# Attention features and a gated feed-forward on one core: tied issue for the gate stage's late work, earlier x rows, fill pieces between the last pairs' products

## The chip, the cores and the metric

The kernel runs on one core of a Trainium2 chip, in one launch. The metric is device time in microseconds; the time before is the median of three runs. A second number, the span, is the time from the first to the last instruction in one profiled execution. Both are lower when better.

## The reference, cut to what matters

```python
def phi(x):                                    # x: [8, 8, 576, 64]
    proj = x @ w_phi                           # [64, 128]
    proj = proj - max(abs(proj), axis=-1)
    return concat([exp(proj), exp(-proj)])
q_p, k_p = phi(q), phi(k)
kv  = einsum('bhsf,bhsd->bhfd', k_p, v);  z = sum(k_p, axis=2)
num = einsum('bhsf,bhfd->bhsd', q_p, kv); den = einsum('bhsf,bhf->bhs', q_p, z) + 1e-06
x   = (num / den) as [4608 tokens, 512]
xn  = x / sqrt(mean(x*x) + 1e-06) * rms_g
g, val = xn @ w_gate, xn @ w_val               # both [512, 1536]
out = (g * sigmoid(g) * val) @ w_out           # [1536, 512]
```

All of it is fp32. Every product is made of three fp32r matmuls over operands that are split into a high and a low half (high by high, high by low, low by high).

## The kernel before, in words

**Three stages follow each other on TensorE.** The *pair stage* (the loop `for i in range(PR + 3)`) treats 32 pairs of heads, each in four steps that are one loop turn apart: `front` (transposes, projection), `mid` (exponentials, the key-value sums), `back` (the query products into the tiles `nd`, then the denominators through DRAM: `dd`, `dr`, reciprocal, `di`, `rc`) and `last` (`nd` times `rc`, written to the DRAM tensor `xs`). `_merge` lays the pieces of these streams into one sequence by their places between 0 and 1.

**Fill pieces.** The first three of the twelve 128-column groups of both feed-forward weights are kept in SBUF (`fg`, `fv`). Their products with the raw x, not yet normalised, are made while the pair stage runs: x is cut in 18 blocks of 256 tokens; `load_x` fetches one by a DMA on ScalarE's queue (line 145), `fill` splits it into the tile `xo` (ScalarE casts the high half at line 60, VectorE subtracts the low half at line 61), and six units (line 482, 12 matmuls of 256 columns each) multiply it. A unit's sum is copied out by ScalarE (`fo`, line 485) and stored to `gvs`. Until the loop is over a unit writes one of the two PSUM tiles of the pool `ps_f` (`fp`); afterwards one of three tiles `sm`. Units are handed out after the streams of a turn by a quota, and all that is left after the loop.

**The gate stage** has 9 blocks of 512 tokens (`bk`). In each, `gv` makes nine column groups j: 12 matmuls for the gate and 12 for the value (line 605), then `hidden` (ScalarE's `sl`, line 588, VectorE's `h`, line 590, a store to `hs`). I call one such group of 24 matmuls a column pair. Three more groups a block come from the fills: `raw_load` fetches `gvr` (line 612), `gv_raw` multiplies it by the row scale `ri` (line 616) and calls `hidden`. Value sums have three PSUM tiles (`gp`); gate sums have three others (`gq`), except in block 0, where they use the two `fp` tiles that the fills use too. The next block's x is fetched (line 145), squared and summed by `prep` (lines 150 to 154, two matmuls with ones at 159 and 160, square root at 162, reciprocal at 163, scaling at 165) and split by `parts` into `xb`. The decoding of w_out (`_decode`, lines 48 to 55) and the making of the output operands (`split_o`, lines 636 to 647, from loads `wc<-wos`) also run here. During block 0 `load_gv` (line 581) loads the weights of columns j + 1 on ScalarE's queue and splits them: high on ScalarE, low on GpSimd.

**The output stage** multiplies `hs` by w_out with seven products per 2 by 2 block (line 777).

**What sets the order.** The program is written out in Python order, and the Tile scheduler then reorders each engine's instructions by a timing model of its own, as dependencies allow. Each engine runs its list in that order, so an instruction that waits holds what stands behind it. `late()` is the kernel's means against early placement: each instruction that it encloses, on ScalarE, VectorE or GpSimd, is made to stand behind the latest instruction written so far on its engine (those that were themselves enclosed are skipped). Before the change it encloses the decoding, the fills' splits, the reciprocal and scaling in `back` and `last`, and the first block's `prep`.

Of the kernel before, what the change touches and what calls it, by code (L numbers as in the profile page):

```python
# [8 lines left out]
F32 = mybir.dt.float32  # L9
# [54 lines left out]
def _merge(streams):  # L64


    todo = []
    for n, st in enumerate(streams):
        for i, piece in enumerate(st):
            at = (i + 0.5) / len(st)  # L70
            if isinstance(piece, tuple):
                at, piece = piece
            todo.append((at, n, i, piece))
    for _, _, _, piece in sorted(todo, key=lambda t: t[:3]):
        piece()


def _spread(pieces, a, b):
    return [(a + (b - a) * (n + 0.5) / len(pieces), p) for n, p in enumerate(pieces)]
# [3 lines left out]
def kernel(ctx: ExitStack, tc: tile.TileContext, q, k, v, w_phi,  # L83
# [13 lines left out]
    J1 = 3  # L97
    T = 512
    NB = N // T
# [48 lines left out]
    def prep(bk, x, pool, name):  # L148
        ss = xm.tile([128, T], F32, name="ss", bufs=1)
        nc.scalar.activation(ss, x[:, 0], AF.Square)  # L150
        for c in range(1, NC):
            sq = xm.tile([128, T], F32, name="sq", bufs=1)
            nc.scalar.activation(sq, x[:, c], AF.Square)
            nc.gpsimd.tensor_tensor(ss, ss, sq, ALU.add)
        sp = pool.tile([128, T], F32, name=name)
        sh = xm.tile([128, T], F32R, name="sq", bufs=1)
        sl = xm.tile([128, T], F32R, name="sl", bufs=1)
        _split(nc, sh, sl, ss, lo_eng=nc.gpsimd)
        nc.tensor.matmul(sp[:, 0:T], ones, sh, start=True, stop=False)
        nc.tensor.matmul(sp[:, 0:T], ones, sl, start=False, stop=True)  # L160
        ri = rip.tile([128, T], F32, name="ri")
        nc.scalar.activation(ri, sp[:, 0:T], AF.Sqrt, scale=1.0 / DM, bias=eps)
        nc.vector.reciprocal(ri, ri)  # L163
        for c in range(NC):
            nc.vector.scalar_tensor_tensor(x[:, c], x[:, c], g[:, c:c + 1], ri, ALU.mult, ALU.mult)  # L165
        return ri

    def parts(bk, x, ri):
        xhl = xops[bk % len(xops)].tile([128, 2, NC, T], F32R, name="xb")
        for c in range(0, NC, 2):  # L170
            _split(nc, *(a[:, c:c + 2] for a in (xhl[:, 0], xhl[:, 1], x)), lo_eng=nc.gpsimd)
        return xhl[:, 0], xhl[:, 1], ri

    ps_f = ctx.enter_context(tc.tile_pool(name="ps_f", bufs=2, space=PSUM))
# [5 lines left out]
    @contextmanager  # L180
    def late():

        ins = nc.cur_bb.bb.instructions
        n = len(ins)
        with ExitStack() as es:
            for eng in LATE:
                for i in reversed(ins[-300:]):
                    if i.engine == eng and i.name not in waiting:
                        es.enter_context(tc.issue_after(i))
                        break  # L190
            yield
        waiting.update(i.name for i in nc.cur_bb.bb.instructions[n:])
# [82 lines left out]
    def load(pr):  # L275
        b, hp = divmod(pr, NP)
        h0 = 2 * hp
        kt = ld.tile([128, 2, T0, D], F32, name="kt")
        qt = ld.tile([128, 2, T0, D], F32, name="qt")
        for dst, src in ((kt, k), (qt, q)):  # L280
            nc.sync.dma_start(out=dst.rearrange("p h t d -> p h (t d)"),
                              in_=src[b, h0:h0 + 2, 0:SM, :].rearrange("h (p t) d -> p h (t d)", t=T0))
        rb = ld.tile([128, 2, D], F32, name="rb")
        vm, vr = vms[pr % 3], vrs[pr % 3]
        for i, src in enumerate((k, q)):
            nc.sync.dma_start(out=rb[:, i], in_=src[b, h0:h0 + 2, SM:S, :])
        for hh in range(2):
            nc.sync.dma_start(out=vm[:, hh, :, 0:D], in_=v[b, h0 + hh, 0:SM, :].rearrange("(p t) d -> p t d", t=T0))
            nc.sync.dma_start(out=vr[hh * 64:(hh + 1) * 64, hh, 0:D], in_=v[b, h0 + hh, SM:S, :])
        st[pr] = dict(kt=kt, qt=qt, rb=rb, hp=hp, b=b, vm=vm, vr=vr, kv=kvs[pr % 2])  # L290
# [174 lines left out]
    fills, ended = [], []  # L465
# [23 lines left out]
    PR = B * NP  # L489
    early, decs_late = decode_jobs()  # L490
    decs = decode_pieces(early, dec)
    RES = 6 * J1 * 2
    units, here = [], []
    dq = quota = 0.0

    def load_x():
        while fills and len(here) < (1 if held else 2):
            bk = fills.pop(0)
            here.append((bk, fetch(bk, TF, nc.scalar)))

    def landed():
        if here:
            units.extend(fill(*here.pop(0)))

    load(0)
    nc.sync.dma_start(out=g, in_=rms_g.rearrange("(c p) -> p c", p=128))
    load(1)
    for i in range(PR + 3):
        streams = []
        if i < PR:  # L510
            streams.append(_spread(front(i), -0.2, 0.7))
        if 0 <= i - 1 < PR:
            streams.append(_spread(mid(i - 1), -0.2, 1.1))
        if 0 <= i - 2 < PR:
            streams.append(back(i - 2))
        if 0 <= i - 3 < PR:
            streams.append(last(i - 3))
        dq += 1
        dl, decs = decs[:int(dq)], decs[int(dq):]
        dq -= int(dq)  # L520
        streams.append(dl)
        _merge(streams)

        if i == PR - 3:
            with late():
                ri0 = prep(0, x0, ps_f, "fp")
        if len(units) <= 3:
            landed()
        if len(units) + (len(fills) + len(here)) * J1 * 2 > RES:
            quota += (N // TF * J1 * 2 - RES) / (PR - 4)  # L530
            nf = int(quota)
            quota -= nf
            now, units[:] = units[:nf], units[nf:]
            _merge([now])
        if i == PR - 5:
            x0 = fetch(0)
            held.append(x0)
        if not PR - 5 <= i < PR - 3:
            load_x()
        if i + 2 < PR:  # L540
            load(i + 2)
# [51 lines left out]
    def gv(bk, j):  # L593
        if bk == 0 and j + 1 < JN:
            load_gv(j + 1)
        xh, xl, _ = xb[bk]
        r = []
        for wi in range(2):
            gp = ps_g.tile([128, 512], F32, name="gp") if wi else ps_h.tile([128, 512], F32, name="gq") if bk else ps_f.tile([128, T], F32, name="fp")
            i = 0  # L600
            pl = place(wi, j)
            for c in range(NC):
                a, al = pl[0][:, c], pl[1][:, c]
                for w, e in ((a, xh), (a, xl), (al, xh)):
                    nc.tensor.matmul(gp[:, 0:T], w, e[:, c], start=(i == 0), stop=(i == 3 * NC - 1))  # L605
                    i += 1
            r.append(gp[:, 0:T])
        hidden(bk, J1 + j, *r)
# [6 lines left out]
    def gv_raw(bk, j, r):  # L615
        nc.vector.tensor_tensor(r, r, xb[bk][2].unsqueeze(1).broadcast_to([128, 2, T]), ALU.mult)  # L616
        hidden(bk, j, r[:, 0], r[:, 1])
# [21 lines left out]
    def split_o(kp, pool, wt):  # L639
        w, t = wt  # L640
        sub = lambda o, a, b: nc.vector.tensor_tensor(t[:, o], a, b, ALU.subtract)  # L641
        sub(0, w[:, 3], w[:, W11])
        sub(2, w[:, W22], w[:, 3])
        sub(1, w[:, W22], t[:, 0])
        sub(3, w[:, W21], t[:, 1])
        wh = pool.tile([128, 7, DH], F32R, name=f"wh{kp}")
        wl = pool.tile([128, 7, DH], F32R, name=f"wl{kp}")
        _split(nc, wh[:, 0:3], wl[:, 0:3], w[:, 0:3])
        _split(nc, wh[:, 3:7], wl[:, 3:7], t)
        return wh, wl  # L650
# [9 lines left out]
    for bk in range(NB):  # L660
        for n, j in enumerate(LAST if bk == NB - 1 else range(JN)):
            gv(bk, j)
            m, k = divmod(n, JN // J1)
            if k == 1:
                gv_raw(bk, m, raw)
            if k == 2 and (m + 1 < J1 or bk + 1 < NB):
                raw = raw_load(bk, m + 1) if m + 1 < J1 else raw_load(bk + 1, 0)
            if n == 1 and bk + 1 < NB:
                xn = fetch(bk + 1)
            if n == JN // 3 and bk + 1 < NB:  # L670
                xb[bk + 1] = parts(bk + 1, xn, prep(bk + 1, xn, *((ps_f, "fp") if bk else (ps_g, "gp"))))
            if bk and n % 2 == 0 and decs:
                decs.pop(0)()
            if wot and n % 4 == 0:
                wos_ops.append(split_o(len(wos_ops), rg, wot))
                wot = None
            if not decs and not wot and len(wos_ops) < PRE and n % 4 == 1:
                wot = fetch_o(len(wos_ops))
# [170 lines left out]
```

## Time and profile before

| | us |
|---|---|
| median of three runs (1323.54, 1328.35, 1331.91) | 1328.35 |
| the profiled execution's own time | 1328.31 |
| its span | 1326.5 |
| TensorE busy in the span | 1281.4 |
| TensorE idle in the span | 45.1 |
| pair stage, up to the last query product | 0 to 492.9 |
| fills left over, block 0 of the gate stage among them | 492.9 to 611.2 |
| gate stage, rest | 611.2 to 1059.9 |
| output stage | 1059.7 to 1326.5 |

Times in the profile are counted from the first instruction. A row of the view of waits names the engine that sat idle, the tile and line it was about to write, and after the arrow what it waited for. In a list of stretches each engine's busy time is followed by its count of instructions; PEclk is the share of TensorE's clock that was granted.

### The profile page before, as it was taken

To read this page: it belongs to the slowest core of one execution; us is meant where nothing else is said; L and a number is where in the kernel's file an instruction comes from. 1 tells how busy PE (TensorE), PEld (TensorE's weight loads), DVE (VectorE), ACT (ScalarE), POOL (GpSimd) and SP (SyncE) were. 2 spreads that over 40 slices of the span, in tenths; PEclk is the share of its full clock that TensorE was granted. 3 is DMA by queue.
4 is the path that set the end of the run, shared out by engine and by line. 5 is a ranking of instruction groups with operands and counts; after the bars stand their busy time and mean duration, and the time that the engine had idled before them with its cause. 6 is when DMAs were issued, how large, how long until landed. Compare 5 with 4: busy or idle time off the path is not lost. (4 is left out here: it accounts for less than half of the span.)

```text
span 1326.5 us, 24218 instructions
## 1 busy us (share of the span) xinstructions
PE 1281.4 (97%) x8886; PEld 1189.3 (90%) x8886; DVE 864.4 (65%) x1228; ACT 701.8 (53%) x1472; POOL 624.8 (47%) x580
## 2 busy tenths in 40 slices
PE   7989999999999998999999999999999999999998
PEld 7989999999999997998888877777888899999998
DVE  7889887888788854113365764656442777678773
ACT  6878886887778874344243332433431444444442
POOL 4666665665566765002321313223310277777773
PEclk9999999999999999999999999999999999999999
DMA  5445575656656337544444535444423544544441
GB/s 161 128 126 151 162 183 172 166 158 169 171 160 190 103 122 222 176 136 136 149 152 140 170 113 178 160 153 136 158 79 124 179 136 144 159 128 154 152 141 48
DMA packets 198229, 197.13 MB, mean 149 GB/s; under 512 B 69024, under 2 KB 154912, under 8 KB 198112
## 3 DMA queue, kind: packets, MB, share of 16 engines
q1 hardware_dynamic: 179104, 181.44, 44.9%
q10 hardware_dynamic: 19008, 14.16, 3.7%
q8 instruction: 70, 1.15, 0.4%
q14 instruction: 47, 0.39, 0.1%
HBM read 126.04 MB, written 69.50 MB: 147 GB/s over the span
## 5 line engine op out<-in xcount | busy, mean ns | idle before, releaser
L388 POOL TENSOR_TENSOR ql<-eq,qh 128x256 fp32r<-128x256 f32 x256 | 217.6, 881 | 55.7 <-issue 30.9
L605 PE MATMUL gp<-xb,wv 128*128 128x512 f32 x648 | 157.8, 392 | 7.3 <-DVE h L590 7.2
L605 PEld LDWEIGHTS gp<-xb,wv 128*128 128x128 f32 x648 | 120.7, 188 | 35.6 <-DVE h L590 11.0
L54 POOL TENSOR_TENSOR wa<-raw,wa 128x192 f32<-128x192 f32 (+1 forms) x112 | 66.4, 613 | 163.4 <-DVE wa L52 94.9
L605 PE MATMUL gq<-xb,wg 128*128 128x512 f32 x576 | 138.5, 390 | 1.4 <-ACT sl L588 1.4
L359 PE MATMUL acc<-vm,ek 128*128 128x65 f32 x1024 | 131.2, 270 | 0.0
L605 PEld LDWEIGHTS gq<-xb,wg 128*128 128x128 f32 x576 | 108.1, 188 | 24.2 <-ACT sl L588 1.8
L359 PEld LDWEIGHTS acc<-vm,ek 128*128 128x128 f32 x1024 | 127.5, 194 | 0.4 <-ACT ek L346 0.2
L323 DVE TENSOR_REDUCE mx<-pp 128x4 f32<-128x512 f32 (+1 forms) x160 | 100.8, 631 | 28.4 <-PE pp L321 26.5
L590 DVE TENSOR_TENSOR h<-sl,gp 128x512 f32<-128x512 f32 x81 | 55.1, 682 | 78.6 <-PE gp L605 50.2
L588 ACT ACTIVATE sl<-gq 128x512 f32<-128x512 f32 x72 | 42.7, 594 | 114.4 <-PE gq L605 85.2
L384 ACT ACTIVATE qh<-sm 128x512 fp32r<-128x512 f32 (+1 forms) x192 | 97.4, 507 | 0.0
L61 POOL TENSOR_TENSOR xb<-x,xb 128x1024 fp32r<-128x1024 f32 x18 | 46.6, 2609 | 105.8 <-ACT xb L60 105.8
L319 PE MATMUL pp<-wh,th 128*128 128x256 f32 x288 | 88.5, 309 | 4.8 <-ACT th L60 1.5
L383 ACT ACTIVATE eq<-sm 128x512 f32<-128x512 f32 x128 | 78.5, 613 | 13.0 <-PE sm L372 9.7
L616 DVE TENSOR_TENSOR gvr<-gvr,ri 128x1024 f32<-128x1024 f32 x27 | 34.9, 1291 | 77.0 <-DMA gvr<-gvs 77.0
L321 PE MATMUL pp<-wh,tl 128*128 128x256 f32 x288 | 84.6, 300 | 0.1
L320 PE MATMUL pp<-wl,th 128*128 128x256 f32 x288 | 81.3, 283 | 0.0
L605 PE MATMUL gp<-xb,fv 128*128 128x512 f32 x324 | 78.1, 390 | 0.0
L346 ACT ACTIVATE ek<-yk 128x512 f32<-128x512 f32 x128 | 75.3, 650 | 1.1 <-DVE yk L326 1.1
L605 PE MATMUL gq<-xb,fg 128*128 128x512 f32 x288 | 70.9, 396 | 1.9 <-ACT sl L588 1.9
L605 PEld LDWEIGHTS gp<-xb,fv 128*128 128x128 f32 x324 | 61.0, 188 | 13.0 <-DVE h L590 0.3
(210 smaller groups left out, 3829.9 us busy)
## 6 DMA issues: line engine op xcount, KB each, us to landing
hs<-h SPq DMA_DIRECT2D x108, 256.0 KB
ht<-hs SPq DMA_DIRECT2D x18, 1536.0 KB
gvs<-fo SPq DMA_DIRECT2D x108, 128.0 KB
gvr<-gvs SPq DMA_DIRECT2D x27, 512.0 KB
rc<-di SPq DMA_DIRECT2D x32, 288.0 KB
x<-xs ACTq DMA_DIRECT2D x18, 512.0 KB
x<-xs SPq DMA_DIRECT2D x9, 1024.0 KB
kt<-in_k_dram SPq DMA_DIRECT2D x32, 256.0 KB
```

The source lines that it names most:

```text
L54: nc.gpsimd.tensor_tensor(a[:, h], lf[:, h], a[:, h], ALU.mult)
L319: nc.tensor.matmul(o, th[:, cs], wh, start=True, stop=False)
L320: nc.tensor.matmul(o, th[:, cs], wl, start=False, stop=False)
L321: nc.tensor.matmul(o, tl[:, cs], wh, start=False, stop=True)
L323: nc.vector.tensor_reduce(mx[:, 0:2 * m], pp[:, 0:2 * m], axis=AX.X, op=ALU.max, apply_absolute_value=True)
L346: nc.scalar.activation(e[h][:, sg], y["k", h], AF.Exp, scale=1.0 - 2.0 * sg)
L359: nc.tensor.matmul(acc[:, sg, h], e[h][:, sg, j], vm[:, h, j], start=False, stop=(h == 1 and j == T0 - 1))
L383: nc.scalar.activation(ei[:, sg], yi, AF.Exp, scale=1.0 - 2.0 * sg)
L384: nc.scalar.activation(hi[:, sg], yi, AF.Exp, scale=1.0 - 2.0 * sg)
L388: nc.gpsimd.tensor_tensor(lo[:, sg, cs], ei[:, sg, cs], hi[:, sg, cs].bitcast(F32), ALU.subtract)
L590: nc.vector.tensor_tensor(h, sl, vr, ALU.mult)
L605: nc.tensor.matmul(gp[:, 0:T], w, e[:, c], start=(i == 0), stop=(i == 3 * NC - 1))
```

## The change

It makes five edits, all of order or of buffers; the arithmetic and the number of instructions on each engine stay the same.

1. `gv_raw`, the later blocks' `prep` and `split_o` are enclosed in `late()`.
2. The next block's x is fetched after column pair 0 instead of 1, and `prep` and `parts` are written after pair 2 instead of 3.
3. In the last two turns of the pair loop a new stream of 8 and 10 calls of `more` lies between 0 and 0.64 of the turn; each makes one fill unit, and splits and loads further x blocks as needed.
4. The quota no longer hands out units in those two turns.
5. The gate sums of block 0 use the three `gp` tiles that the value sums use, no longer the `fp` tiles.

```diff
+    def more():
+        if len(units) <= 3:
+            landed()
+        if units:
+            units.pop(0)()
+        load_x()
...
+        if i > PR:
+            streams.append(_spread([more] * (8 if i == PR + 1 else 10), 0, 0.64))
         _merge(streams)
...
-        if len(units) + (len(fills) + len(here)) * J1 * 2 > RES:
+        if i <= PR and len(units) + (len(fills) + len(here)) * J1 * 2 > RES:
...
-            gp = ps_g.tile([128, 512], F32, name="gp") if wi else ps_h.tile([128, 512], F32, name="gq") if bk else ps_f.tile([128, T], F32, name="fp")
+            gp = ps_g.tile([128, 512], F32, name="gp") if wi else ps_h.tile([128, 512], F32, name="gq") if bk else ps_g.tile([128, 512], F32, name="gp")
...
             if k == 1:
-                gv_raw(bk, m, raw)
+                with late():
+                    gv_raw(bk, m, raw)
...
-            if n == 1 and bk + 1 < NB:
+            if n == 0 and bk + 1 < NB:
                 xn = fetch(bk + 1)
-            if n == JN // 3 and bk + 1 < NB:
-                xb[bk + 1] = parts(bk + 1, xn, prep(bk + 1, xn, *((ps_f, "fp") if bk else (ps_g, "gp"))))
+            if n == 2 and bk + 1 < NB:
+                with late():
+                    rin = prep(bk + 1, xn, *((ps_f, "fp") if bk else (ps_g, "gp")))
+                xb[bk + 1] = parts(bk + 1, xn, rin)
...
             if wot and n % 4 == 0:
-                wos_ops.append(split_o(len(wos_ops), rg, wot))
+                with late():
+                    wos_ops.append(split_o(len(wos_ops), rg, wot))
```

Lines after the new function are numbered 7 to 13 higher in the changed kernel: 588, 590 and 616 become 597, 599 and 625.

**Where the order moves.** The first place is VectorE at the end of the pair stage. `kv1l` is the last pair's key-value sum, `nd` the scaling of a pair that is done, `xo` the low half of a fill block. Before:

```order
L61 TENSOR_TENSOR kv1l<-acc,kv1h 128x4x65
L433 RECIPROCAL dr<-dr 128x9
L450 TENSOR_TENSOR nd<-nd,rc 64x576
L451 TENSOR_TENSOR nd<-nd,rc 64x576
L616 TENSOR_TENSOR gvr<-gvr,ri 128x1024
L61 TENSOR_TENSOR xo<-x,xo 128x512 x2
```

and now:

```order
L61 TENSOR_TENSOR kv1l<-acc,kv1h 128x4x65
L433 RECIPROCAL dr<-dr 128x9
L61 TENSOR_TENSOR xo<-x,xo 128x512 x2
L450 TENSOR_TENSOR nd<-nd,rc 64x576
L451 TENSOR_TENSOR nd<-nd,rc 64x576
L433 RECIPROCAL dr<-dr 128x9
L599 TENSOR_TENSOR h<-sl,gp 128x512
```

The fill block's low half stands ahead of the two scalings, and the first multiplication of `gvr` has left this place.

The second place is VectorE in the middle of the gate stage, the 29th to the 32nd `h` of a column pair (block 3). `wc` and `wl` belong to `split_o`. Before:

```order
L55 TENSOR_TENSOR wa<-wp,wa 128x256
L641 TENSOR_TENSOR wc<-wc 128x256
L590 TENSOR_TENSOR h<-sl,gp 128x512
L590 TENSOR_TENSOR h<-sl,gvr 128x512
L616 TENSOR_TENSOR gvr<-gvr,ri 128x1024
L590 TENSOR_TENSOR h<-sl,gp 128x512
...
L590 TENSOR_TENSOR h<-sl,gp 128x512
L163 RECIPROCAL ri<-ri 128x512
L641 TENSOR_TENSOR wc<-wc 128x256 x2
L61 TENSOR_TENSOR wl_12014<-wc,wh_12013 128x768
L165 SCALAR_TENSOR_TENSOR x<-x,g,ri 128x512 x4
```

and now, from the 29th to the 33rd:

```order
L55 TENSOR_TENSOR wa<-wp,wa 128x256
L599 TENSOR_TENSOR h<-sl,gp 128x512
L625 TENSOR_TENSOR gvr<-gvr,ri 128x1024
L599 TENSOR_TENSOR h<-sl,gvr 128x512
L599 TENSOR_TENSOR h<-sl,gp 128x512 x3
L625 TENSOR_TENSOR gvr<-gvr,ri 128x1024
L163 RECIPROCAL ri<-ri 128x512
L599 TENSOR_TENSOR h<-sl,gvr 128x512
L165 SCALAR_TENSOR_TENSOR x<-x,g,ri 128x512 x4
```

From one multiplication of `gvr` to the next there are now always three `h` of column pairs, where before there were two to four, and the work on `wc` is gone from here: the first four output operands now stand around the 60th to the 73rd `h`, in blocks 6 to 8.

The third place is ScalarE at the end of the pair stage: `wg`, `wv` are the weight tiles of block 0 (their number is the column group), `wc` their loads. Before:

```order
L60 CAST wv_1_9025<-wc 128x512
L485 COPY fo<-fp 128x256
L425 ACTIVATE nd<-sm,epsd 65x288 x2
L581 DMA wc<-wgs 128x4x128
L485 COPY fo<-fp 128x256
L581 DMA wc<-wvs 128x4x128
L485 COPY fo<-fp 128x256
L60 CAST xo<-x 128x512 x2
L60 CAST wg_2_9027<-wc 128x512
L60 CAST wv_2_9029<-wc 128x512
L485 COPY fo<-fp 128x256
L145 DMA x<-xs 128x4x256
```

and now:

```order
L60 CAST wv_1_9025<-wc 128x512
L485 COPY fo<-fp 128x256
L145 DMA x<-xs 128x4x256
L485 COPY fo<-fp 128x256
L425 ACTIVATE nd<-sm,epsd 65x288 x2
L590 DMA wc<-wgs 128x4x128
L590 DMA wc<-wvs 128x4x128
L60 CAST wg_2_9027<-wc 128x512
L485 COPY fo<-fp 128x256
L60 CAST wv_2_9029<-wc 128x512
L485 COPY fo<-fp 128x256
L590 DMA wc<-wgs 128x4x128
```

The load of the next x block moves ahead of the weight loads, the casts of `xo` have left (they now stand ahead of the first weight's cast), and the casts of the third weights stand between the fills' copies.

## The prediction

> **What bounds the kernel now.** I read the busy shares first, then the same by stretches that follow the stages.
>
> ```profile
> PE 1281.4 (97%) x8886; PEld 1189.3 (90%) x8886; DVE 864.4 (65%) x1228; ACT 701.8 (53%) x1472; POOL 624.8 (47%) x580
> ```
>
> ```profile
> 493.70:560.00 66.30, 60.23 (x459) 58.34 (x458) 21.73 (x21) 29.14 (x67) 21.65 (x14) 0.97 0.67 208
> 560.00:610.00 50.00, 50.00 (x402) 49.18 (x402) 6.90 (x10) 20.06 (x48) 7.47 (x6) 1.00 0.44 140
> 610.00:760.00 150.00, 150.00 (x669) 124.44 (x668) 82.94 (x105) 56.84 (x95) 43.34 (x39) 1.00 0.45 150
> 760.00:930.00 170.00, 159.48 (x683) 128.22 (x682) 99.03 (x139) 57.77 (x98) 45.56 (x48) 0.99 0.44 147
> 930.00:1060.00 130.00, 130.00 (x576) 107.72 (x576) 63.21 (x67) 40.00 (x58) 22.29 (x11) 1.00 0.40 136
> ```
>
> TensorE (PE) is the bound. In these rows (time, busy time and count of PE, PEld, DVE, ACT and POOL, PE's granted clock, DMA) it has no gap in three stretches of the part that the change reorders; two have holes: 493.7 to 560 (fills and block 0) and 760 to 930 (blocks 3 to 6). Whatever the change gains, it gains there. The waits of TensorE in these two name who was late:
>
> ```profile
> PE fp L482 <- DVE xo L61: 4.7, 1, 4.7
> PE sm L423 <- DVE kv1l L61: 2.3, 1, 2.3
> PE sm L482 <- ACT fo L485: 1.4, 1, 1.4
> ```
>
> ```profile
> PE gp L605 <- DVE h L590: 7.2, 7, 2.1
> PE gq L605 <- ACT sl L588: 3.2, 2, 1.9
> ```
>
> In the second, VectorE's (DVE) own waits show why `h` was late, and ScalarE's (ACT) why `sl` was:
>
> ```profile
> DVE gvr L616 <- DMA gvr<-gvs: 22.7, 8, 6.6
> DVE wa L55 <- POOL wa L54: 17.4, 12, 6.2
> DVE wc L641 <- DMA wc<-wos: 17.4, 6, 5.9
> DVE h L590 <- DMA hs<-h: 6.7, 3, 2.5
> ```
>
> ```profile
> ACT sl L588 <- DVE h L590: 36.1, 13, 5.8
> ACT ss L150 <- DMA x<-xs: 29.1, 3, 11.7
> ```
>
> VectorE was busy 99.0 us there and waited 22.7 + 17.4 + 17.4 + 6.7 = 64.2 us: 163 of 170. So its list, with its waits, was as long as the stretch, and `h` fell behind until the three `gp` tiles ran out. One of these holes, on VectorE:
>
> ```profile
> 769.84 0.68 DVE L590 TENSOR_TENSOR h<-sl,gp 128x512 f32<-128x512 f32 x1
> 770.44 0.69 DVE L590 TENSOR_TENSOR h<-sl,gvr 128x512 f32<-128x512 f32 x1
> 777.70 1.23 DVE L616 TENSOR_TENSOR gvr<-gvr,ri 128x1024 f32<-128x1024 f32 x1 [6.58 <-DMA gvr<-gvs]
> 778.84 0.68 DVE L590 TENSOR_TENSOR h<-sl,gp 128x512 f32<-128x512 f32 x1
> ```
>
> The `h` at 778.84 needs nothing of `gvr`; it stood behind it for 6.6 us, and TensorE with it once its tiles were used up.
>
> **Part 1: the late ties and the earlier x in the gate stage.** What can be gained at most is counted from the rows: 930 to 1060 runs 576 matmuls in 130.00 us, 0.2257 us each. 683 at that rate are 154.2 us; the stretch took 170. The loss is 15.8 us: 10.5 idle, the rest restarts and a time at half clock:
>
> ```profile
> 790.00:795.00 5.00, 5.00 (x15) 0.66 0.13 52
> ...
> 504.00:508.00 4.00, 3.88 (x20) 0.57 1.00 322
> ```
>
> ```profile
> 789.89 2.42 PE L605 MATMUL gq<-xb,fg 128*128 128x512 f32 x7 [1.85 <-ACT sl L588]
> ```
>
> The first of the two stretches costs 5 × (1 − 0.66) = 1.7 us and follows TensorE's 1.85 us wait in the third row; the other costs 4 × 0.43 = 1.7 us, right behind the 4.7 us wait on `xo`. I count both as consequences of the waits. [...]
>
> In the new order the multiplication of `gvr` stands right behind the `h` of its own column pair, its load is issued as soon as the buffer is free, and three column pairs lie between them: 3 × 5.44 us from these rows of the chain, against the 6.6 us that the longest such wait lasted.
>
> ```profile
> 1054.44 2.72 PE gq L605 x12
> 1057.16 2.72 PE gp L605 x12
> ```
>
> The 22.7 us of `gvr` waits go. The `wc` work (17.4 us of waits) leaves the stretch. VectorE's list there is then at most 99.0 + 17.4 + 6.7 = 123.1 us for some 156: it no longer falls behind. On ScalarE the squares of x stand behind the `sl` of pair 2 and the x load is issued before the next block begins, as soon as the split of the last x frees the tile, so the 29.1 us of waits on x go too.
>
> Next late is the chain of `prep`; its rows, and those of `split_o`, are these.
>
> ```profile
> L163 DVE RECIPROCAL ri<-ri 128x512 f32<-128x512 f32 x8 | 26.8, 3349 | 1.2 <-ACT ri L162 1.2
> L165 DVE SCALAR_TENSOR_TENSOR x<-x,g,ri 128x512 f32<-128x512 f32 x32 | 21.9, 747 | 0.3
> ...
> L61 DVE TENSOR_TENSOR wl<-wc,wh 128x768 fp32r<-128x768 f32 (+1 forms) x12 | 14.0, 1176 | 1.0 <-ACT wh L60 0.9
> ...
> L641 DVE TENSOR_TENSOR wc<-wc 128x256 f32<-128x256 f32 x24 | 11.6, 505 | 32.3 <-DMA wc<-wos 32.2
> ```
>
> ```profile
> 515.97 0.63 ACT L153 ACTIVATE sq<-x 128x512 f32<-128x512 f32 x1 [0.61 <-POOL ss L154]
> ```
>
> ```profile
> 517.14 1.29 POOL L154 TENSOR_TENSOR ss<-ss,sq 128x512 f32<-128x512 f32 x1
> ```
>
> ```profile
> L61 POOL TENSOR_TENSOR xb<-x,xb 128x1024 fp32r<-128x1024 f32 x18 | 46.6, 2609 | 105.8 <-ACT xb L60 105.8
> ```
>
> Between the `sl` of pair 2, which can come 2.6 pairs into a block, and the matmul at 159 lie four squares, three sums on GpSimd (POOL) and a cast, 4 × 0.63 + 3 × 1.29 + 0.6 = 7.0 us, then 1.3 for the low half that 160 needs, and the handovers. In TensorE's new list 159 stands behind 4.8 of the block's pairs, 2.2 pairs or 12 us later. Then follow VectorE's reciprocal and scaling, 3.35 + 4 × 0.75 = 6.4 us, and two `xb` splits on GpSimd, 5.2 us; counted from a square root 5 pairs in, with a `gvr` and two `h` between, they end near pair 7.5 of 9. Where this cover fails, the missing microseconds are paid once a block, eight times.
>
> The operands of w_out move to blocks 6 to 8. VectorE's worst list between two `h` is there one `gvr` (1.23), three `wc` (0.5 each), one `wl` (1.2), the reciprocal and two `h` (0.7 each), about 8.7 us, more than a pair's 5.44. With three tiles a value sum may wait for its `h` 2.5 pairs, 13.6 us, so this is hidden; a load as late as the longest before (5.9) brings it to 14.6 and a microsecond shows. All waits on `wc` were 32.2 us; 930 to 1060 has 130 − 63 = 67 us free on VectorE. I leave 1.5 us of the 15.8: gain 14.3, bounds 0 and 15.8.
>
> **Part 2: the end of the pair stage.** The loss in 493.7 to 560 is 6.1 us idle plus 1.7 of half clock, 7.8 us. The 4.7 us wait is this:
>
> ```profile
> 495.72 2.71 DVE L450 TENSOR_TENSOR nd<-nd,rc 64x576 f32<-64x576 f32 x1 [5.35 <-DMA rc<-di]
> 498.44 1.75 DVE L451 TENSOR_TENSOR nd<-nd,rc 64x576 f32<-64x576 f32 x1
> 500.22 2.17 DVE L616 TENSOR_TENSOR gvr<-gvr,ri 128x1024 f32<-128x1024 f32 x1
> 502.32 3.43 DVE L61 TENSOR_TENSOR xo<-x,xo 128x512 fp32r<-128x512 f32 x2
> ```
>
> A fill block's split stood behind two scalings that waited for DRAM and behind a `gvr`. Now it stands ahead of all three, some ten microseconds before TensorE reaches the block. The 18 units in the last two turns are the same units, so TensorE's work is the same; products of block 0 now stand among them and use the `gp` tiles. The 2.3 us wait on `kv1l` stays: the list up to it is the same.
>
> What the new order costs is on ScalarE, which now casts `xo` before the first weights and has the third weights' casts between the fills' copies:
>
> ```profile
> 493.12 0.38 ACTq L581 DMA_DIRECT2D wc<-wgs  x1
> ...
> 496.25 1.14 ACT L60 CAST xo<-x 128x512 fp32r<-128x512 f32 x2
> 498.33 0.62 ACT L60 CAST wg<-wc 128x512 fp32r<-128x512 f32 x1 [0.94 <-DMA wc<-wgs]
> ```
>
> The casts put the first `fo` some 1.5 us later; TensorE loses about 1. A weight load takes 498.33 − 493.12 = 5.2 us; a copy behind its cast is needed about when it comes, 0 to 1.5 us lost. Three tiles for block 0 instead of five need each `h` within 5.44 us of its product; `gvr`, two `h` and their semaphores are under 3. I leave 1.8 us, gain 6.0; bounds 7.8 gained, and five loads of 5.2 us all exposed, 26 lost.
>
> **The sum.** 14.3 + 6.0 = 20.3 us. The profiled execution took 1328.31 us, beside a median of 1328.35, so nothing is to be corrected: 1328.3 − 20.3 = 1308.0, with a span near 1306.2.
>
> **Rivals.** *VectorE falls behind again in blocks 6 to 8.* The operands of w_out are now packed into fifteen pairs with their loads just ahead. For it: the 32.2 us of waits. Against: the free 67 us. If each of the five operands made there opens one hole as long as the longest on `h` above, 2.1 us: 1308.0 + 10.5 = 1318.5, or less where fewer do.
>
> *The gate stage stays as it is*, the ties changing what VectorE waits for and not how long its list is: it shares its time with GpSimd, as 2.71 us and 1.75 us for two equal scalings (rows below 495.72) hint, and the waits on `wa` move up. Against: 40 us of waits have no cause in the new order. Then 1328.3 − 6.0 = 1322.3. That the ties do nothing at all is ruled out by the lists.
>
> *Slower: weight casts hold the fills' copies.* In the last two turns all units still have only two `fp` tiles, and on ScalarE each weight cast stands ahead of a copy that frees one. If all five remaining loads of block 0 are exposed, TensorE stands 5 × 5.2 us and pays 1.7 of half clock each time, 34.5 instead of 7.8: 1328.3 + 26.7 − 14.3 = 1340.7. It decides from (7.8 + 14.3) / 5 = 4.4 us exposed per load. Against it: the loads are issued one or two groups ahead, and 24 fill matmuls and 12 of a product, 5.6 us, lie between.
>
> **How the numbers follow.** Forecast 0.73 (own range 1303 to 1313), VectorE behind again 0.12 (a quarter of it below 1315), gate unchanged 0.09, slower 0.06. All losses gone would give 1328.3 − 15.8 − 7.8 = 1304.7, and the runs before lie up to 4.8 us from their median, so the range goes from 1302 to 1319, which leaves out the last two cases and little else. Faster by over 1% is below 1315.1, about what a measurement of this kernel can tell from no change: 0.73 and a quarter of 0.12, 0.76. Within 1%: 0.09 + 0.09 = 0.18. Slower: 0.06.
>
> **What would show it.** Right: no TensorE wait on `h` or `sl` between 760 and 930, VectorE's waits on `gvr` near zero, no wait on `xo`, full clock from 500 to 900; the `kv1l` wait still there. Wrong: waits on `fo` near 500 (ScalarE's casts), at line 159 (the chain of `prep`), or on `h` behind `wc` after 930.

## The result, and the profile after

| | kernel before | changed kernel |
|---|---|---|
| median of 6 runs each, one chip | 1329.23 us (1323.54 to 1334.87) | 1311.77 us (1310.44 to 1319.19) |
| ratio, 95% interval | 1 | 0.9881 [0.9844, 0.9918] |
| profiled execution (span) | 1328.31 us (1326.5) | 1319.19 us (1315.7) |

Faster by 1.2%: 17.5 us by the two medians, where 20.3 were forecast. The time is 3.8 us above the 1308.0 of the forecast and inside the range. The profiled execution of the changed kernel is the slowest of its six, so the stages are compared from a point that both share: the first product behind the wait on `kv1l`. First before, then after, from the timeline of TensorE:

```profile
487.96 0.40 PE L423 MATMUL sm<-qh,kv1l 128*128 128x288 f32 x1 [2.26 <-DVE kv1l L61]
```

```profile
490.95 0.40 PE L423 MATMUL sm<-qh,kv1l 128*128 128x288 f32 x1 [1.58 <-DVE kv1l L61]
```

From there to the end it is 1326.5 − 487.96 = 838.5 us before and 1315.7 − 490.95 = 824.8 after: 13.8 us less. The 3.0 us that the changed kernel is behind at that point belong to work that the change leaves as it was: up to there both have run the same 3797 matmuls.

The profile after by stretches (time, busy time and count of PE, PEld, DVE, ACT and POOL, granted clock, DMA):

```profile
490.95:560.00 69.05, 62.07 (x410) 56.70 (x411) 21.80 (x26) 32.41 (x64) 24.40 (x18) 0.98 0.61 184
...
610.00:760.00 150.00, 150.00 (x731) 127.13 (x731) 62.91 (x92) 54.19 (x99) 44.89 (x42) 1.00 0.46 154
760.00:930.00 170.00, 170.00 (x752) 140.81 (x751) 83.19 (x123) 63.46 (x106) 48.34 (x50) 1.00 0.42 144
930.00:1047.00 117.00, 117.00 (x518) 96.92 (x517) 70.85 (x89) 41.57 (x57) 23.75 (x11) 1.00 0.46 153
```

The row from 760 to 930 us is the whole gain. It had 683 matmuls and 10.5 us of holes before; now 752 and none. At the 0.2257 us of the prediction 752 are 169.7 us: a loss of 0.3 us where 15.8 stood. The first row has 7.0 us of holes, where 6.1 stood. VectorE's waits from 760 to 930 us show what changed on the engine that was late:

```profile
DVE h L599 <- PE gp L614: 60.2, 19, 5.0
DVE wp L50 <- ACT wa L48: 13.1, 9, 2.1
DVE wa L55 <- POOL wa L54: 7.9, 12, 1.1
```

The first row reads the other way round from before: VectorE waits for TensorE's next product. The waits on `gvr` and `wc` are gone, and of those on `hs` 0.2 us are left.

TensorE's waits from 490.95 to 560 us:

```profile
PE fp L482 <- ACT fo L485: 7.0, 5, 4.3
PE sm L423 <- DVE kv1l L61: 1.6, 1, 1.6
```

`xo` is gone, as forecast, and a wait of the same size on the fills' copies `fo` has come. The longest, 4.29 us, ends at 534.29. ScalarE (ACT) before it:

```profile
509.36 0.37 ACTq L590 DMA_DIRECT2D wc<-wgs  x1
...
510.38 0.37 ACT L485 COPY fo<-fp 128x256 f32<-128x256 f32 x1 [7.75 <-DMA gvs<-fo]
...
520.98 0.84 ACT L485 COPY fo<-fp 128x256 f32<-128x256 f32 x2
530.25 0.62 ACT L60 CAST wg<-wc 128x512 fp32r<-128x512 f32 x1 [8.43 <-DMA xs<-nd]
530.78 0.61 ACT L60 CAST wv<-wc 128x512 fp32r<-128x512 f32 x1
533.46 0.37 ACTq L590 DMA_DIRECT2D wc<-wgs  x1
533.87 0.37 ACT L485 COPY fo<-fp 128x256 f32<-128x256 f32 x1 [2.48 <-POOL wv L61]
```

The cast of the fifth pair's weights waits 8.43 us for a store of the last attention pair: those weights are put where that pair's numerators `nd` stood. The copy that gives TensorE its tile back stands behind. Earlier, the copy at 510.38 stood 7.75 us behind the issue of a weight load, which waited until transfers from SP's queue had landed; the profile names a store of `gvs` as the last of them, and writes the wait of an issue at the next instruction behind it. SP's stores and transfers were late because of what SP and VectorE show:

```profile
495.34 0.43 SPq L427 DMA_DIRECT2D dd<-nd  x1
504.05 0.32 SPq L456 DMA_DIRECT2D xs<-nd  x1
...
506.43 0.27 SPq L427 DMA_DIRECT2D dd<-nd  x1
...
526.68 0.32 SPq L456 DMA_DIRECT2D xs<-nd  x1
```

```profile
500.30 1.96 DVE L450 TENSOR_TENSOR nd<-nd,rc 64x576 f32<-64x576 f32 x1 [5.77 <-issue]
502.27 1.75 DVE L451 TENSOR_TENSOR nd<-nd,rc 64x576 f32<-64x576 f32 x1
515.39 0.22 DVE L433 RECIPROCAL dr<-dr 128x9 f32<-128x9 f32 x1 [11.37 <-DMA dr<-dd]
...
525.12 0.75 DVE L450 TENSOR_TENSOR nd<-nd,rc 64x576 f32<-64x576 f32 x1 [5.14 <-DMA rc<-di]
```

SP issues nothing for 8 us, until the scaling of the last pair but one is done at 504.0; the last pair's `dd` stands behind, then its `dr`, `di` and `rc`, each through DRAM. VectorE idles 22 us ahead of the rows shown (for the first 5.77 us the profile names no cause), and what stands behind it or SP is late.

### The profile page after: what moved, and what is told of

It is laid out like the page before. It is cut to its first block, busy times and chain, and to the rows that moved or that the text cites. A ratio compares the mean times of both kernels' runs of the same rounds, so it can differ in the third digit from the quotient of the medians.

```text
span 1315.7 us, 24224 instructions
## 1 busy us (share of the span) xinstructions
PE 1279.0 (97%) x8886; PEld 1190.3 (90%) x8886; DVE 839.8 (64%) x1228; ACT 705.3 (54%) x1472; POOL 623.7 (47%) x580
## 4 chain that ended last, share of the span: by engine, by line
PE 85%; DVE 5%; DMA 5%; ACT 2%; issue 1%; SPq 1%; POOL 0%; ACTq 0%; POOLq 0%; DVEq 0%
PE gp L614 18%; PE gq L614 15%; PE gd L790 6%; PE gy L790 6%; PE gz L790 6%; PE sm L482 6%; PE acc L359 6%; PE fp L482 5%; PE sm L423 4%; PE fp L790 3%; PE fp L423 2%; PE pp L321 2%; PE pp L319 2%; PE pp L320 2%; PE sm L372 2%; PE sm L306 2%
## 5 line engine op out<-in xcount | busy, mean ns | idle before, releaser
L154 POOL TENSOR_TENSOR ss<-ss,sq 128x512 f32<-128x512 f32 x27 | 34.9, 1291 | 80.9 <-ACT sq L153 80.9
```

## The experiments

All runs are timed against the kernel before on the same chip; the ratio has its 95% interval. Waits and spans are those of the one profiled execution.

### The gate stage's edits alone

The fill pieces are taken out of the changed kernel again; the ties and the earlier x stay:

```diff
...
-            streams.append(_spread([more] * (8 if i == PR + 1 else 10), 0, 0.64))
...
-        if i <= PR and len(units) + (len(fills) + len(here)) * J1 * 2 > RES:
+        if len(units) + (len(fills) + len(here)) * J1 * 2 > RES:
...
-            gp = ps_g.tile([128, 512], F32, name="gp") if wi else ps_h.tile([128, 512], F32, name="gq") if bk else ps_g.tile([128, 512], F32, name="gp")
+            gp = ps_g.tile([128, 512], F32, name="gp") if wi else ps_h.tile([128, 512], F32, name="gq") if bk else ps_f.tile([128, T], F32, name="fp")
```

> The late ties and the earlier x of the gate stage alone; the end of the pair stage as in the kernel before. Theory now held (the whole gain is the gate stage's, the fill pieces bring nothing): within 3 us of the changed kernel's 1311.8, no TensorE wait on h or sl between 760 and 930 us, the wait on xo of about 4.7 us still there. Rival (the prediction's sum: the fill pieces bring 6.0): 1315 to 1318, some 6 us above the changed kernel. Another: without the fill pieces block 0 comes in another order and the ties meet another list; then waits on h stay and the time is above 1320.

0.9853 [0.983, 0.9876], 1314.92 us. No wait of TensorE between 560 and 1060 us; from 485 to 560:

```profile
PE fp L482 <- DVE xo L61: 2.4, 1, 2.4
PE sm L423 <- DVE kv1l L61: 2.3, 1, 2.3
PE sm L482 <- ACT fo L485: 1.7, 2, 1.1
```

These edits carry the result by themselves. In these runs the kernel before has a median of 1335.54 us, so the ratio is compared and not the time: 0.9853 of 1329.2 is 1309.7, within the 3 us of the theory held. But the wait on `xo`, which the fill pieces are to remove, is 2.4 us here and not 4.7: the gate stage's edits had taken a part of it already.

### The fill pieces alone

The other half: ties and x fetch as before, `more`, quota and `gp` tiles as changed.

> The fill pieces, their quota and the gp tiles of block 0 alone; the gate stage as in the kernel before. Theory now held: 1327 to 1331, no difference that shows against 1329.2; the wait on xo gone and waits of TensorE on fo of 4 us or more between 497 and 535 us in its place; waits on h of about 7 us between 760 and 930 still there. Rival (the prediction's sum): 1329.2 - 6.0 = 1323.2.

0.9964 [0.9951, 0.9977], 1330.31 us: 4.8 us less than before (3.1 to 6.5). My theory of no difference falls here, and the prediction's 6.0 is inside the interval. TensorE's waits from 485 to 560, and from 560 to 1060:

```profile
PE sm L423 <- DVE kv1l L61: 2.3, 1, 2.3
PE fp L482 <- ACT fo L485: 2.2, 3, 1.3
PE gp L614 <- ACT sl L597: 1.5, 1, 1.5
```

```profile
PE gp L614 <- DVE h L599: 10.5, 8, 2.3
PE gq L614 <- ACT sl L597: 0.5, 1, 0.5
```

The gate stage is as bad as before. At the end of the pair stage, without the wait on `kv1l`, 3.7 us of waits stand where 6.1 were; that is half of the 4.8 us, and for the rest the trace shows no cause. The cast that costs 8.43 us in the changed kernel waits 1.94 here, with a copy of `fo` ahead of it:

```profile
526.66 0.37 ACT L485 COPY fo<-fp 128x256 f32<-128x256 f32 x1
528.97 0.62 ACT L60 CAST wg<-wc 128x512 fp32r<-128x512 f32 x1 [1.94 <-DMA xs<-nd]
```

So the fill pieces bring something alone and the same pieces meet another list when the ties are in.

### The tie on gvr alone, and everything of the gate stage but that tie

```diff
-                gv_raw(bk, m, raw)
+                with late():
+                    gv_raw(bk, m, raw)
```

Against the kernel before, this one edit:

> Only the late tie on the multiplication of gvr, nothing else of the change. Theory (VectorE's list was a few us short of the stretch, and the 22.7 us of gvr waits are what made it too long): the list in 760 to 930 falls from 163 to about 140 of 170 us, the waits on h go, and most of the 15.5 us come: 1314 to 1318. Rival (each tie brings its share, since the squares of x on ScalarE and the wc work on VectorE are late by themselves): a third, 22.7 of 64.2 us, about 1324, with sl waits left on TensorE.

0.9874 [0.9852, 0.9896], 1318.79 us. The second kernel has the tie on the squares of x with the earlier fetch, and that on `split_o`, and `gv_raw` as before:

> The gate stage's edits without the tie on the multiplication of gvr: the tie on split_o, the tie on the squares of x and the earlier x load only; the end of the pair stage as before. Theory (what counts is how long VectorE's list with its waits is, and any tie that shortens it from 163 to below some 150 of 170 us will do): 17.4 us of wc waits and 6.7 on hs go, the list is about 139, no waits on h, a ratio near 0.986. Rival (what counts is the one wait that stands ahead of a ready h, the gvr load's): holes of 1 to 2.3 us on h stay, a ratio near 0.995.

0.9874 [0.9845, 0.9904], 1316.69 us. VectorE from 760 to 930 us, its waits and then the stretch, first with the tie on `gvr` alone:

```profile
DVE wc L641 <- DMA wc<-wos: 22.3, 6, 5.8
DVE wa L55 <- POOL wa L54: 15.0, 15, 1.4
...
DVE h L590 <- PE gp L605: 2.2, 1, 2.2
```

```profile
760.00:930.00 170.00, 169.46 (x747) 139.82 (x746) 105.15 (x146) 63.60 (x107) 48.51 (x49) 1.00 0.50 160
```

and without that tie:

```profile
DVE h L590 <- PE gp L605: 24.9, 6, 5.0
DVE gvr L616 <- DMA gvr<-gvs: 20.7, 4, 5.7
```

```profile
760.00:930.00 170.00, 170.00 (x751) 140.77 (x750) 88.80 (x128) 64.48 (x108) 52.48 (x50) 1.00 0.44 146
```

Either half removes the holes, the first all but 0.5 us of them. In the second the `gvr` waits are still there, 20.7 us, as before the change (22.7), and TensorE waits for nothing. It isn't one wait ahead of a ready `h` that counted but the length of the list: VectorE's time to spare (its waits for TensorE's `gp`) is none before, 2.2 us with one tie, 24.9 with the other two, 60.2 with all. With 2.2 it is at the edge: one 0.5 us wait on `sl` is left. Counted as in the prediction (busy time and the waits on loads, stores and the decoding), the list was 163 us before and is 152 with the one tie, where 140 were expected, 137 with the other two and 104 with all.

### Another place for the weights

In the changed kernel, the memory of the fifth and of the sixth pair's weights is exchanged:

```diff
-    wps = {j: own(f"m_w{j}") for j in (4, 5)}
+    wps = {j: own(f"m_w{j}") for j in (5, 4)}
```

> The changed kernel with the memory of the fifth and the sixth column pair's weights of block 0 exchanged, so that the sixth pair's, which are made a pair later, lie over the last pairs' numerators. Theory (the 4.3 us wait of TensorE on fo and the half clock behind it come from the cast of the fifth pair's weights waiting for the last pair's store): both go, 1311.8 - 4.3 - 1.7 = 1306, and ScalarE shows no wait on xs<-nd above 1 us near 530. Rival (the fo copies are late for another reason, the queue of stores behind the wait on SP): 1310 to 1313, the wait on fo near 530 stays.

0.9875 [0.9853, 0.9897], 1317.64 us; the waits on `fo` are 5.5 us. The scheduler now casts the sixth pair's weights first, and these wait as the fifth's did:

```profile
534.00 0.62 ACT L60 CAST wg<-wc 128x512 fp32r<-128x512 f32 x1 [5.37 <-DMA xs<-nd]
```

The edit did not take the dependence away, so it decides nothing.

### The change again, more tiles, and the numerators apart

> The changed kernel as it is, beside the runs that follow and those of the kernel with the gate stage's edits alone (0.9853 of the kernel before, on one chip). If the fill pieces bring 4.8 us in the company of the ties as they did alone (0.9964): 0.982. If they bring nothing there: 0.985. If they cost (the stretch from 485 to 560 us lost 11.9 us in the changed kernel against 8.3 with the gate edits alone): 0.988.

0.9884 [0.9849, 0.9918], 1316.72 us, waits on `fo` 6.1 us. By its middle the fill pieces cost something in the company of the ties, but the interval holds the 0.9853 of the gate edits alone: whether they gain or lose a little there is not shown.

```diff
-            fp = ps_s.tile([128, 512], F32, name="sm") if ended else ps_f.tile([128, T], F32, name="fp")
+            fp = ps_s.tile([128, 512], F32, name="sm") if ended or tail and wi else ps_f.tile([128, T], F32, name="fp")
...
         if i > PR:
+            tail.append(1)
```

> The changed kernel, with the value halves of the last two turns' fill pieces in the three PSUM tiles sm that the pairs leave free, so that these pieces have five tiles instead of two. Theory (TensorE waits on fo because each piece must have one of two fp tiles back, and a late weight cast on ScalarE stands ahead of the copy that frees it): the waits on fo in 485 to 560 us, 7.0 us in the changed kernel, fall below 2, and the time by 4 to 7 us against the changed kernel of the same chip. Rival (five tiles only put off the same wait, since ScalarE's list with its waits is as long as the stretch): the waits on fo stay above 4 us and the time within 2.

0.9919 [0.9887, 0.9951], 1322.53 us: not faster, and by its middle 5.8 us slower than the change run again. Waits on `fo` are 3.1 us, between the two theories, but the scheduler put most of block 0's products behind the fills (33 of their 216 matmuls come before the last fill, where 108 did), and a new wait came at block 1's sums of squares, at 618 us:

```profile
PE gp L159 <- ACT sq L60: 5.1, 1, 5.1
```

Inconclusive on the tiles.

```diff
-    ndp = a_ctx.enter_context(tc.tile_pool(name="a_nd", bufs=2))
...
     dec = a_ctx.enter_context(tc.tile_pool(name="a_dec", bufs=1))
+    ndp = a_ctx.enter_context(tc.tile_pool(name="a_nd", bufs=2))
...
-    wps = {j: own(f"m_w{j}") for j in (4, 5)}
+    wps = {j: own(f"m_w{j}") for j in (5, 4)}
```

> The changed kernel with the pool of the numerators (nd) on top of the pair stage's memory, where no weights of block 0 are put, and the fifth and sixth pair's weights exchanged, so that the fifth's lie over memory that is free early. Theory: the fifth weights' cast no longer waits for the last store of xs (8.4 us on ScalarE), the 4.3 us wait on fo near 530 us goes and the half clock behind it, 5 to 6 us less than the changed kernel of the same chip. Rival (the list of ScalarE waits next for the weight loads, whose tile or queue is late by as much): a wait on fo of 2 us or more between 515 and 535 stays and the time is within 3 us.

0.9882 [0.9849, 0.9916], 1317.09 us. The wait of the cast on the store is gone, and 4.8 us on `fo` are back elsewhere. ScalarE then:

```profile
510.53 0.37 ACTq L590 DMA_DIRECT2D wc<-wgs  x1
510.93 1.28 ACT L597 ACT_TABLE_LOAD   x1 [3.50 <-DMA gvr<-gvs]
...
515.03 0.37 ACTq L590 DMA_DIRECT2D wc<-wvs  x1
515.43 0.62 ACT L60 CAST wg<-wc 128x512 fp32r<-128x512 f32 x1 [2.62 <-DMA x<-xs]
```

The rival held: take one cause away and the next stands in its place, here the issue of a weight load that waits until transfers from SP's queue have landed.

### The weight loads from GpSimd's queue

```diff
-            nc.scalar.dma_start(out=w[:, wi], in_=src[:, (J1 + j) * 128:(J1 + j + 1) * 128].rearrange("(c p) j -> p c j", p=128))
+            nc.gpsimd.dma_start(out=w[:, wi], in_=src[:, (J1 + j) * 128:(J1 + j + 1) * 128].rearrange("(c p) j -> p c j", p=128))
```

This one edit was made to three kernels. To the changed kernel:

> The changed kernel with one edit: block 0's weight loads are issued from GpSimd's queue and not from ScalarE's. Theory (ScalarE's list is as late as it is because these loads are issued in it, and an issue waits until an earlier DMA, one that SP holds up behind the last pairs' stores of xs, has landed; the copies of fo behind it wait too): ScalarE shows no wait above 1 us that ends on gvr or x or gvs in 500 to 525 us, the waits on fo fall from 6 to 7 us to about 4, the one near 530 us that the last store causes; the time falls by about 3 us against the changed kernel (0.986 of before). Rival (the issue is no more than one of many waits of a list that waits anyway for the loads to land): waits on fo of 6 us or more, 0.988 or above.

To the changed kernel with the numerators apart:

> The two edits together: the numerators apart from the weights' memory (with the fifth and sixth weights exchanged) and the weight loads issued from GpSimd's queue. Theory: with both causes of waits on ScalarE gone, the waits on fo in 485 to 560 us fall below 2 us and the stretch's loss from 11.7 to below 6; 6 us less than the changed kernel, 0.984. Rival (each cause taken away shows the next one, as with the numerators alone): waits on fo of 4 us and more stay, 0.987 to 0.989.

To the kernel with the gate stage's edits alone:

> The gate stage's edits alone with the weight loads issued from GpSimd's queue, the end of the pair stage otherwise as before. There the waits left in 485 to 560 us are kv1l 2.3, xo 2.4 to 3 and fo 1.5. If the issues on ScalarE make the xo casts and copies late: the xo and fo waits fall below 2 together and the time is 0.982 to 0.984. If xo is late because VectorE waits for the last pairs' reciprocals: no change, 0.985 to 0.988.

On the changed kernel 0.9916 [0.9886, 0.9947]; with the numerators apart 0.9914 [0.9886, 0.9941]; on the gate edits alone 0.9918 [0.989, 0.9946]. None is better, and the third is slower: the gate edits alone gave 0.9853, and the intervals do not meet. The waits on `fo` are 10.1, 4.9 and 3.3 us. The first kernel's ScalarE, and the second's VectorE:

```profile
527.82 0.60 ACT L597 ACTIVATE sl<-gp 128x512 f32<-128x512 f32 x1 [13.20 <-DVE xo L61]
```

```profile
512.45 0.22 DVE L433 RECIPROCAL dr<-dr 128x9 f32<-128x9 f32 x1 [10.69 <-DMA dr<-dd]
...
520.42 0.75 DVE L450 TENSOR_TENSOR nd<-nd,rc 64x576 f32<-64x576 f32 x1 [7.18 <-DMA rc<-di]
```

Now ScalarE waits for a split of `xo` on VectorE, and VectorE for the last pair's round trips through DRAM. My theory that the issues on ScalarE are the cause falls; they handed on a wait. Nine of the 18 runs of these three kernels have a mean clock below the lowest of the change run again (down to 0.990 against 0.994). The second kernel's trace shows where it went in one execution: from 485 to 560 us the granted clock is 0.93, against 1.00 in the same kernel without this edit. In the first it is 0.50 from 528.4 to 531.8 us. In the third the mean clock of the profiled execution is 0.992, against 0.995 with the gate edits alone: by an estimate from these and the two spans 1318.9 × 0.008 − 1311.3 × 0.005 = 4.0 us, beside 2 us more of waits, where its span is 7.6 us longer. Why more of the clock goes there stays open.

### The last two pairs without their division

```diff
-            if c == 1:
+            if c == 1 and pr < PR - 2:
...
+            if pr >= PR - 2:
+                d.update(nd=nd, rc=None)
+                return
...
+                if rc is None:
+                    nc.vector.tensor_copy(xt[64:128], nd[1][0:64])
```

In the changed kernel this leaves out, for the last two pairs, `dd`, `dr`, `di`, `rc`, the reciprocal and the two scalings; their x is not divided.

> The changed kernel without the division of the last two pairs: their four small DMAs through DRAM (dd, dr, di, rc), the reciprocal and the two scalings are left out, and a copy of one half and the store of xs stay. Theory (the root of every wait on fo in 485 to 560 us are these round trips: VectorE waits for them some 25 to 30 us there, SP waits for VectorE with the stores of xs, and loads, copies and casts stand behind SP): the waits on fo fall from 6 to 7 us to below 1.5, the stretch's loss from 11.7 to about 5 with the 2.3 us on kv1l left, and the time is 6 to 7 us below the changed kernel's, 0.983 to 0.984 of before. Rival (block 0's weight loads, of 5 us each through two tiles, are too slow by themselves for the new order): waits of 4 us and more on fo stay, 0.987 or above.

0.9817 [0.9789, 0.9844], 1307.02 us: some 9 us below the change run again (0.9884), where 6 to 7 were expected; the intervals do not meet. TensorE from 485 to 560 us:

```profile
485.00:560.00 75.00, 73.08 (x521) 68.63 (x521) 21.26 (x26) 41.75 (x89) 30.68 (x25) 1.00 0.61 189
```

```profile
PE sm L423 <- DVE kv1l L61: 1.6, 1, 1.6
PE fp L488 <- ACT fo L491: 0.3, 1, 0.3
```

The same casts, weight loads and two `fp` tiles, and 0.3 us of waits on `fo`, at full clock. The division of the last two pairs, with its round trips, is the root; the weight loads by themselves are quick enough. How much of it is the round trips and how much the reciprocals and scalings on VectorE, this edit doesn't separate.

## Why the prediction was right, and where it was not

**Gate stage: right, in size and cause.** Forecast 14.3 of 15.8, measured 15.5. The argument that VectorE's list with its waits (163 of 170 us) was too long is what the two halves show: each shortens it by another part and each suffices. The wait on `gvr`, which the prediction puts first, need not go for this: with the other two ties the holes went as well. The 1.5 us left for late `wc` were not needed. The waits on x on ScalarE, 29.1 us, are gone, and line 159 waits nowhere.

**End of the pair stage: wrong.** Forecast 6.0 gained of 7.8. In the profile after, the stretch loses 7.0 us idle and 3.5 × (1 − 0.55) = 1.6 at half clock, 8.6:

```profile
534.50:538.00 3.50, 3.50 (x19) 3.50 (x19) 0.92 (x2) 3.22 (x8) 1.28 (x1) 0.55 0.97 293
```

That is 0.8 more than before, and of the signs named for being right, no wait on `xo` came, but full clock from 500 to 900 us did not. The step that failed is the sentence "a copy behind its cast is needed about when it comes, 0 to 1.5 us lost": it priced a weight cast by its own load, 5.2 us, and did not ask what else the cast waits for. One cast waits for the memory under its tile, which the last pair gives back only after its round trips (8.43 us); and the issue of a load waits for transfers that SP held up (7.75 us). The slower rival named the right place, casts ahead of copies with two tiles, with another cause and at a quarter of its price: 8.6 and not 34.5 us. What is late next was answered for `xo` alone: behind it stood the same reciprocals and scalings.

**The sum.** With the measured terms 1328.3 − 15.5 + 0.8 = 1313.6 (1311.77 measured). From the first product behind `kv1l` to the end the two traces differ by 13.8 us, where 15.5 − 0.8 = 14.7 should; 0.9 us have no name. That the forecast is only 3.8 us off although one term missed by 6.8 is in part luck: the gate stage gave 1.2 us more than forecast, and the median after lies 1.8 us under the sum of the measured terms. The time also holds something outside the span: it is 1.8 us above the span before, 3.5 in the profiled execution after and 2.1 to 3.3 in others of that kernel. Why is open.

**The half clock.** Right: from 760 to 930 us the clock is 1.00 now that the 1.85 us wait is gone, where it was 0.66 from 790 to 795 us before; as far as this shows, the dip was a consequence of the waits. Five of the experiments' kernels (the tie on `gvr` alone, the gate edits without it, the numerators apart without and with the weight loads from GpSimd's queue, and the last two pairs without their division) have at most one wait of 0.5 us from 760 to 930 us, and 1.00 there too.

**VectorE behind again, and the gate stage unchanged** did not come: 930 to 1047 has no hole, and the ties shortened the list. On the equal scalings that the second of them starts from, the trace before shows this: beside an idle GpSimd they took 0.74 to 0.75 us, beside one that was busy all the time 0.74 to 2.71.

## What to carry to other kernels

When an engine's busy time and waits fill a stretch, count the waits that can leave its list; here it mattered little which of them went, once the engine had time to spare. When a wait is removed, follow the removed one back to its root before pricing what comes next: here `xo`, `fo`, weight casts and DMA issues were all late behind one chain of small transfers, and moving one of them changed the name in the table and gained nothing. And an edit's worth alone (4.8 us) is not its worth beside another one.

## What the runs showed of the hardware

The length of a wait of TensorE of up to 3.0 us did not decide whether half clock followed. In one execution (the kernel without the tie on `gvr`) it waited 3.0 us on `xo`, and full clock followed (first row), and 2.3 us on `kv1l`, and half clock followed (second row):

```profile
509.30:512.60 3.30, 3.30 (x27) 3.21 (x28) 1.57 (x1) 0.17 (x1) 2.71 (x2) 1.00 0.93 304
493.50:497.00 3.50, 3.50 (x16) 3.50 (x17) 0.21 (x1) 1.72 (x4) 0.17 (x2) 0.54 0.40 124
```

In the kernel before, 2.26 us were followed by 1.00 (488.0 to 491.5 us) and 1.85 us by 0.66 (790 to 795 us). Behind five longer waits the clock of the next 3.4 to 3.5 us was at most 0.67: 0.51 behind 4.65 us (the kernel before), 0.55 behind 4.29 (the changed kernel), 0.67 behind 3.8 (the change run again), 0.50 behind 9.6 and 0.50 behind 4.9 (the weight loads from GpSimd's queue, on the changed kernel and with the numerators apart); for two more, 4.1 us with the tie on `gvr` alone and 5.1 with more tiles, no row shows the clock behind them. The times of one kernel go with its mean clock, though not strictly: of 17 executions of the kernel before on one chip the fastest took 1329.15 us at 0.994 and the slowest 1339.42 at 0.989, but one at 0.988 took 1335.59.

On ScalarE the issue of a weight load waited for an earlier transfer, and the engine stood with it: 3.50 us with the numerators apart, until a load of `gvr` that SP had issued had landed (the issue at 510.53), and 7.75 us in the changed kernel, until a store of `gvs` had (the issue at 509.36).
